# Two feed-forward layers, each taken in two halves of its inner features through one ring of 28 weight slots

## The chip, the cores and the metric

One core of one Trainium2 chip runs the whole program. The metric is the device time of one execution in microseconds (us); lower is better. The kernel before was timed three times, and one further execution was profiled.

## What is computed

Attention with a position bias over 4 batches, 8 heads and 576 positions gives `x`, 2304 tokens of 512 features. Two feed-forward layers follow:

```python
def _moe_ref(x, w_in, w_out):            # d_ff 2048
    h = x @ w_in
    return (h * np.clip(h + 3.0, 0.0, 6.0) / 6.0) @ w_out

def _moe2_ref(x, w_gate, w_val, w_out):  # d_ff 1536
    gate = 1.0 / (1.0 + np.exp(-(x @ w_gate)))
    return (gate * (x @ w_val)) @ w_out
```

## The kernel before

**Stages.** The bias is built and attention runs (to about 367 us), then layer 1 and layer 2. The change touches the two layers and the weight loader alone. Both layers walk over 6 tiles of 384 tokens (`TW`, `NTILE`).

**Layer 1** goes for each tile over 16 blocks `f` of 128 inner features. For a block, `project` issues 12 matmuls (each operand is split in a high and a low part, so 4 chunks times 3 products), `hardswish` makes `g` (ScalarE L535, VectorE L536), `split_g` cuts it in `gh` (ScalarE L566) and `gl` (VectorE L567), and `out1` issues 12 matmuls into four PSUM accumulators. `out1` runs two blocks behind `project`, by the list `pend`. At a tile's end `split_x` makes the next tile's `XH` and `XL` (four ScalarE casts L520, four VectorE subtractions L521), the last two `out1` follow, and the accumulators are copied through two `raw` buffers and written to DRAM as `x2` (L623). The projections of blocks 0 and 1 of the first tile are issued within attention.

**Layer 2** has 12 blocks `e` per tile: two projections (gate and value), sigmoid (ScalarE L645), a product (VectorE L646), `split_g`, and `out2`, nine matmuls of 512 columns, one block behind.

**The weights.** 32 parts for layer 1 (`w_in`, `w_out` in turn), 36 for layer 2 (gate, value, out in turn). They come as 64-bit floats of 128x512 and are turned into a high and a low 32-bit part by a `Loader`. One `tick` starts the DMA of coming parts into `raw` (SyncE queue), takes the magnitude of part `i` on ScalarE (L133) and VectorE (L134) into a `z` buffer, puts part `i-1` together in three VectorE operations (L141, L143, L145), and splits part `i-2` into its slot: a cast on ScalarE (L151) and a subtraction on GpSimd (L152). There are four `z` buffers; a `z` is free when GpSimd is done with it. So a part costs two ScalarE, four VectorE and one GpSimd operation.

**When ticks run.** Ten parts are loaded during attention. All others of layer 1 are loaded in the first tile, at 1.7 ticks a block (`TICK1`). Layer 2 starts loading in layer 1's last tile (1.5 ticks a block up to 16, `TICKS`, `TICKN`), and continues in its own first tile at two ticks a block. In all other tiles no weight is loaded: a layer's parts all stay in SBUF.

All engines run in program order, so an instruction that waits holds up those behind it on its engine.

Of the kernel before, what the change touches and what calls it, by code (L numbers as in the profile page):

```python
# [46 lines left out]
LATE = 3  # L47

TICK1 = 17
TICKS, TICKN = 12, 16  # L50
# [46 lines left out]
def block_kernel(ctx: ExitStack, tc: tile.TileContext, q, k, v, mlp, w_in, w_out, w_gate, w_val, w_out2, dist_d,  # L97
# [12 lines left out]
    x2 = [dram.tile([P, 4, TW], F32, name=f"x2_{t}") for t in range(NTILE)]  # L110

    class Loader:
# [6 lines left out]
        def __init__(self, todo, raw_tile=None):  # L119
            self.todo, self.raw_tile = todo, raw_tile or (lambda i: ring("raw"))  # L120
            self.raw, self.z, self.n, self.sent, self.done = {}, {}, 0, 0, 0

        def dma(self, i):
            if i < len(self.todo) and i == self.sent:
                raw = self.raw_tile(i).rearrange("p r f -> p (r f)").bitcast(I32)
                self.raw[i] = raw.rearrange("p (f w) -> p f w", w=2)
                nc.sync.dma_start(raw, self.todo[i][1].bitcast(I32))
                self.sent += 1
# [32 lines left out]
        def tick(self):  # L161
# [5 lines left out]
            for j in range(i, i + (3 if pools else 2)):  # L167
                self.dma(j)
# [4 lines left out]
    slots2, X2, outs, spare = [], [], [], []  # L173
    pools, turn = [], [0]

    def ring(name):
# [3 lines left out]
        turn[0] += 1  # L180
        if pools and turn[0] % 3 == 0:
            return pools[0].tile([P, 2, 512], F32, name="raw")
        return stg.tile([P, 2, 512], F32, name="raw", bufs=2)

    def slot1(i):
        if len(slots) == i:
            slots.append(pools[0].tile([P, 2, 512], F32R, name=f"slot{i}"))
        return slots[i]

    def raw1(i):  # L190

        if pools and i < 32 - 2 * LATE and i % 2:
            return pools[0].tile([P, 2, 512], F32, name=f"slot{32 - LATE + i // 2 % LATE}")
        return ring("raw")

    def todo(where, parts):
        return [((lambda i=i: where(i)), part) for i, part in enumerate(parts)]

    load1 = Loader(todo(slot1, [w[f] for f in range(NF) for w in (w_in, w_out)]), raw1)
    load2 = Loader(todo(lambda i: slots2[i], [w[e] for e in range(NE) for w in (w_gate, w_val, w_out2)]))  # L200

# [235 lines left out]
    with ExitStack():  # L437
# [95 lines left out]
        def hardswish(f, ph):  # L533
            g = (outs if outs else x1)[f % 2][:, 0:TW]
# [8 lines left out]
        for i in range(NSLOT):  # L543
# [5 lines left out]
            if i in (NS // 2 + 1, NS // 2 + 2):  # L549
                f = len(begun)  # L550
                begun[f] = hardswish(f, project(slots[2 * f], pp.tile([P, 2, 512], F32, name="s")[:, 0]))
            if i % EVERY == 0 and i > 10 and load1.n < NPRE:
                with tc.issue_after(last_v[0].ins):
                    load1.whole()
            if i in PRIME:
                load1.tick()
# [4 lines left out]
        pools.append(moe)  # L561
# [7 lines left out]


        def out1(f, g, os):
            gh, gl = g
            sl = slots[2 * f + 1]
            for r, x in ((0, gh), (1, gh), (0, gl)):
                for c in range(4):
                    nc.tensor.matmul(os[c][:, 0:TW], sl[:, r, P * c : P * c + P], x,  # L576
                                     start=(f == 0 and r == 0 and x is gh), stop=(f == NF - 1 and x is gl))

        def load_x2(t):
            nc.sync.dma_start(X2[t % 2], x2[t])  # L580

        for t in range(NTILE):
            os, pend = [], []
            if t == NTILE - 1:
                for i in range(2):
                    w = keep.tile([P, NT], F32R, name=f"x{i}")
                    slots2 += [w[:, 1024 * j : 1024 * j + 1024].rearrange("p (r f) -> p r f", r=2) for j in range(2)]
                slots2 += slots
                for i in range(2, 4):
                    w = keep.tile([P, NT], F32, name=f"x{i}")  # L590
                    X2.append(w[:, 0 : 4 * TW].rearrange("p (c t) -> p c t", c=4))
                    outs.append(w[:, 4 * TW : 4 * TW + 512])
                    spare += [w[:, 512 * j : 512 * j + 512] for j in range(2)]
                load_x2(0)
            for f in range(NF):
                if t == 0:
                    while load1.done < min(2 * f + 2, 2 * NF):
                        load1.tick()
                g = begun.pop(f) if f in begun else hardswish(f, project(slots[2 * f]))
                if f == 0:  # L600
                    os += [mp.tile([P, 512], F32, name=f"o{c}") for c in range(4)]
                pend.append((f, split_g(g), os))
                if t == 0:
                    while load1.n < min(NPRE + 2 + TICK1 * (f + 1) // 10, 2 * NF + 2):
                        load1.tick()
# [84 lines left out]
```

## Time and profile before

| | us |
|---|---|
| median of 3 runs | 1253.83 (1253.34 to 1255.91) |
| the profiled execution: time / span | 1257.99 / 1256.2 |
| TensorE busy | 1201.4 (96%) |
| VectorE busy | 663.4 (53%) |
| ScalarE busy | 538.3 (43%) |
| GpSimd busy | 284.1 (23%) |

A busy share is a mean over all stages: TensorE can be the engine that sets the end in one tile and wait for another engine in the next. So the stages are read one by one.

### The profile page before, as it was taken

The numbers are of one execution on the slowest core, as the hardware profiler recorded it, in microseconds if no ns is written. First come the engines' busy times: TensorE is split into PE (matmuls) and PEld (weight loads), VectorE is DVE, ScalarE is ACT, GpSimd is POOL, SyncE is SP. The second block draws the span as 40 slices with busy tenths as digits, with TensorE's granted clock in tenths as the row PEclk, the third lists the DMA queues.
The fourth block names the chain that finished last, engine by engine and source line by source line (L and its number), as shares of the span: only waits on it lengthen the run. The fifth ranks groups of instructions, "written<-read, shape, count | busy, mean of one in ns | idle before, by whom it ended". The sixth has DMA issues, their size and how long they took to land.

```text
span 1256.2 us, 18666 instructions
## 1 busy us (share of the span) xinstructions
PE 1201.4 (96%) x7302; PEld 1063.9 (85%) x7302; DVE 663.4 (53%) x1312; ACT 538.3 (43%) x1123; POOL 284.1 (23%) x222
## 2 busy tenths in 40 slices
PE   7889999999998899999999998989999999999998
PEld 3367777776777799999999997978999999999998
DVE  8967777777878932323242499795112121221211
ACT  5867777776854432323232454543112121221211
POOL 4925566655424400000000043231000000000000
PEclk9989999999999999999999999989999999999999
DMA  5643635253233200000010342541001010000000
GB/s 167 231 158 97 184 100 178 87 155 112 74 120 130 84 26 1 26 1 26 1 45 16 109 142 93 186 151 59 9 1 51 1 51 1 1 26 1 26 1 26
DMA packets 31160, 92.60 MB, mean 74 GB/s; under 512 B 3552, under 2 KB 6880, under 8 KB 31072
## 3 DMA queue, kind: packets, MB, share of 16 engines
q1 hardware_dynamic: 31072, 91.41, 22.6%
q8 instruction: 57, 0.93, 0.3%
q14 instruction: 31, 0.25, 0.1%
HBM read 71.35 MB, written 20.05 MB: 73 GB/s over the span
## 4 chain that ended last, share of the span: by engine, by line
PE 76%; DVE 14%; issue 5%; ACT 3%; DMA 1%; POOL 1%; SPq 0%; DVEq 0%; ACTq 0%
PE o L576 11%; PE h L528 11%; PE h L530 11%; PE h L529 11%; PE o L633 11%; PE s L280 6%; PE av L370 5%; PE tr L338 4%; DVE z L143 4%; DVE z L134 2%; DVE z L145 2%; PE s L507 2%; PE av L373 1%; DVE z L141 1%; DVE x L502 1%
## 5 line engine op out<-in xcount | busy, mean ns | idle before, releaser
L529 PE MATMUL h<-early,slot 128*128 128x384 f32 x880 | 294.8, 335 | 0.9 <-POOL slot L152 0.9
L528 PE MATMUL h<-early,slot 128*128 128x384 f32 x880 | 295.5, 336 | 0.1
L530 PE MATMUL h<-early,slot 128*128 128x384 f32 x880 | 294.9, 335 | 0.0
L646 DVE TENSOR_TENSOR g<-g,h 128x384 f32<-128x384 f32 x72 | 39.8, 553 | 251.4 <-PE h L530 250.8
L529 PEld LDWEIGHTS h<-early,slot 128*128 128x128 f32 x880 | 165.6, 188 | 3.9 <-POOL slot L152 1.2
L528 PEld LDWEIGHTS h<-early,slot 128*128 128x128 f32 x880 | 165.8, 188 | 3.3 <-ACT slot L151 0.4
L576 PE MATMUL o<-gh,slot 128*128 128x384 f32 x768 | 151.0, 338 | 16.2 <-ACT gh L566 16.2
L530 PEld LDWEIGHTS h<-early,slot 128*128 128x128 f32 x880 | 165.4, 188 | 0.0
L576 PEld LDWEIGHTS o<-gh,slot 128*128 128x128 f32 x768 | 134.0, 188 | 20.8 <-ACT gh L566 20.7
L152 POOL TENSOR_TENSOR slot<-z,slot 128x512 fp32r<-128x512 f32 x64 | 95.0, 1487 | 181.8 <-ACT slot L151 156.6
L536 DVE SCALAR_TENSOR_TENSOR x<-x,h 128x384 f32<-128x384 f32 x94 | 51.9, 552 | 132.9 <-ACT x L535 132.8
L300 ACT ACTIVATE p<-u,stat 128x576 f32<-128x576 f32 x128 | 98.6, 772 | 46.3 <-DVE stat L284 40.6
L280 PE MATMUL s<-k,q 128*128 128x288 f32 x640 | 114.5, 313 | 0.5 <-DVE stat L284 0.3
L633 PE MATMUL o<-slot,gh 128*128 128x512 f32 x396 | 104.5, 399 | 7.2 <-ACT gh L566 7.2
L535 ACT ACTIVATE x<-h,half 128x384 f32<-128x384 f32 x94 | 54.5, 580 | 130.8 <-PE h L530 130.8
L645 ACT ACTIVATE g<-h 128x384 f32<-128x384 f32 x72 | 35.4, 492 | 174.1 <-PE h L530 172.3
L284 DVE CUSTOM_DVE_ANT_0 u<-s,bias 128x576 f32<-128x576 f32 x128 | 93.5, 753 | 16.0 <-PE s L280 12.1
L566 ACT CAST gh<-g 128x384 fp32r<-128x384 f32 x72 | 36.9, 513 | 132.7 <-DVE g L646 132.7
L280 PEld LDWEIGHTS s<-k,q 128*128 128x128 f32 x640 | 91.2, 193 | 2.5 <-DVE stat L284 0.9
L633 PEld LDWEIGHTS o<-slot,gh 128*128 128x128 f32 x396 | 74.0, 190 | 20.4 <-ACT gh L566 8.2
L576 PE MATMUL o<-gl,slot 128*128 128x384 f32 x384 | 83.7, 339 | 2.1 <-DVE gl L567 2.1
L567 DVE TENSOR_TENSOR gl<-x,gh 128x384 fp32r<-128x384 f32 x96 | 59.4, 619 | 43.8 <-ACT gh L566 43.8
(103 smaller groups left out, 1775.7 us busy)
## 6 DMA issues: line engine op xcount, KB each, us to landing
raw<-in_part_dram SPq DMA_DIRECT2D x61, 512.0 KB, 3.5
nbias<-p SPq DMA_DIRECT2D x18, 576.0 KB, 4.5
early<-in_part_dram SPq DMA_DIRECT2D x32, 288.0 KB, 4.3
bias<-nbias SPq DMA_DIRECT2D x16, 576.0 KB, 6.5
vn<-in_part_dram SPq DMA_DIRECT2D x16, 320.0 KB, 3.1
early<-in_part_dram SPq DMA_DIRECT2D x16, 304.0 KB, 3.7
x<-raw SPq DMA_DIRECT2D x12, 384.0 KB, 3.0
x<-x SPq DMA_DIRECT2D x6, 768.0 KB, 4.1
```

What stands on the lines that cost most here:

```text
L152: nc.gpsimd.tensor_tensor(out=slot[:, 1], in0=z, in1=slot[:, 0].bitcast(F32), op=ALU.subtract)
L280: nc.tensor.matmul(ps[:, a, 0:HS], Q[:, q0 : q0 + P], K[:, r, h, HS * a : HS * a + HS], start=(i == 0), stop=(i == len(mm) - 1))
L284: nc.vector.tensor_tensor_reduce(out=halves(u), in0=ps[:, :, 0:HS], in1=halves(bt), op0=ALU.add, op1=ALU.min, scale=-0.125, scalar=3e38, a ...
L300: nc.scalar.activation(probs(t), us.pop(t), AF.Exp, bias=low[n % 2][:, s : s + 1], scale=-1.0, accum_out=sums[n % 3][:, s : s + 1])
L370: nc.tensor.matmul(ps[64 * h : 64 * h + 64, 0:HS], vt[:, 4 * h + g], ptm[:, h, g, cols], start=(g == 0), stop=False)
L528: nc.tensor.matmul(ps[:, 0:TW], wh, XH[:, c], start=(c == 0), stop=False)
L529: nc.tensor.matmul(ps[:, 0:TW], wl, XH[:, c], start=False, stop=False)
L530: nc.tensor.matmul(ps[:, 0:TW], wh, XL[:, c], start=False, stop=(c == 3))
L535: nc.scalar.activation(g, ph, AF.Relu, bias=half, scale=1.0 / 6.0)
L567: nc.vector.tensor_tensor(out=gl, in0=g, in1=gh.bitcast(F32), op=ALU.subtract)
L576: nc.tensor.matmul(os[c][:, 0:TW], sl[:, r, P * c : P * c + P], x, start=(f == 0 and r == 0 and x is gh), stop=(f == NF - 1 and x is gl))
L633: nc.tensor.matmul(os[i], x[:, P * i : P * i + P], sl[:, r], start=(e == 0 and x is gh and r == 0), stop=(e == NE - 1 and x is gl))
```

## The change

One `Loader` takes all 68 parts in order, and a part goes to slot `i % 28` of a ring (`NALL`), 10 slots of which exist from the start and 18 after attention. Each layer runs twice over the six tiles. Pass 1 takes the first half of the inner features (8 blocks in layer 1, 6 in layer 2), pass 2 the rest. In layer 1 pass 1 writes its sums to DRAM (`part_d`); pass 2 reads them back (`take`) and adds them on VectorE while it empties PSUM. In layer 2 pass 1 leaves its sums in SBUF (`acc`) and pass 2 adds into them there. `XH` and `XL` are now made for 24 half tiles in place of 12 tiles. `go_on` gives one tick a block in the first and last half tile of a pass, one every second block between them, as long as the ring has a free slot; in layer 2 one a block. `freed` counts slots that the last half tile of a pass gives back block by block. `raw` buffers for loading are two now; before there were three and some slots not yet in use.

```diff
-LATE = 3
-TICK1 = 17
-TICKS, TICKN = 12, 16
+NALL = 28
...
         def split(self, i):
             if i in self.z:
-                slot, z = self.todo[i][0](), self.z.pop(i)
+                slot, z = slots[i % NALL], self.z.pop(i)
...
-            for j in range(i, i + (3 if pools else 2)):
+            for j in range(i, i + 2):
                 self.dma(j)
...
+        def go_on(freed, to):
+
+            if load.n - 2 < min(NALL + freed, to):
+                load.tick()
...
+        for part2, t in todo:
             os, pend = [], []
...
+            part = take(part_d[t]) if part2 else None
+            for f in range(NH * part2, NH * part2 + NH):
+                while load.done < 2 * f + 2:
+                    load.tick()
...
-                if t == 0:
-                    while load1.n < min(NPRE + 2 + TICK1 * (f + 1) // 10, 2 * NF + 2):
-                        load1.tick()
...
-                    while load2.n < min(TICKS * (f + 1) // 8, TICKN):
-                        load2.tick()
...
+                freed = 2 * NH * part2
                 if t == NTILE - 1:
+                    freed += max(0, 2 * (f - NH * part2 - 1))
+                if f % 2 == 0 or t == 0 or t == NTILE - 1:
+                    go_on(freed, 68)
...
-                evac("AV"[c % 2], two[:, c % 2, 0:TW], os[c][:, 0:TW])
+                if part2:
+                    nc.vector.tensor_tensor(out=two[:, c % 2, 0:TW], in0=os[c][:, 0:TW], in1=part[:, c], op=ALU.add)
+                else:
+                    evac("AV"[c % 2], two[:, c % 2, 0:TW], os[c][:, 0:TW])
                 if c % 2 == 1:
-                    nc.sync.dma_start(x2[t][:, c - 1 : c + 1], two[:, :, 0:TW])
+                    nc.sync.dma_start((x2 if part2 else part_d)[t][:, c - 1 : c + 1], two[:, :, 0:TW])
...
-                if t == 0:
-                    load2.tick()
-                    load2.tick()
...
+                freed = 2 * NF + 3 * NH * part2
+                if t == NTILE - 1:
+                    freed += 3 * (e - NH * part2)
+                go_on(freed, 68)
...
             for i in range(NB):
...
+                o = acc[NB * t + i]
+                if part2:
+                    nc.vector.tensor_tensor(out=o, in0=o, in1=os[i], op=ALU.add)
+                    nc.sync.dma_start(out[TW * t + P * i : TW * t + P * i + P, :], o)
+                else:
+                    evac("AV"[i % 2], o, os[i])
```

The order of VectorE's queue in layer 1's first tile, before, from one block's `hardswish` (L536) to the next:

```order
L536 SCALAR_TENSOR_TENSOR x1_64<-x1_64,h_4420 128x384
L141 TENSOR_SCALAR z_4405<-z_4405 128x512
L134 TENSOR_SCALAR z_4447<-z_4447 128x512
L143 SCALAR_TENSOR_TENSOR z_4405<-slot29_4350,z_4405 128x512
L567 TENSOR_TENSOR gl_4436<-x1_64,gh_4435 128x384
L145 SCALAR_TENSOR_TENSOR z_4405<-slot29_4350,z_4405 128x512
L141 TENSOR_SCALAR z_4447<-z_4447 128x512
L134 TENSOR_SCALAR z_4458<-z_4458 128x512
L143 SCALAR_TENSOR_TENSOR z_4447<-raw_4392,z_4447 128x512
L536 SCALAR_TENSOR_TENSOR x0_63<-x0_63,h_4473 128x384
```

The same place after the change, where the lines are L514 for `hardswish`, L545 for `gl`, and L132, L139, L141, L143 for the four operations of a part:

```order
L514 SCALAR_TENSOR_TENSOR g_4409<-g_4409,h_4410 128x384
L141 SCALAR_TENSOR_TENSOR z_4406<-raw_4362,z_4406 128x512
L545 TENSOR_TENSOR gl_4426<-g_4409,gh_4425 128x384
L143 SCALAR_TENSOR_TENSOR z_4406<-raw_4362,z_4406 128x512
L132 TENSOR_SCALAR z_4448<-z_4448 128x512
L139 TENSOR_SCALAR z_4448<-z_4448 128x512
L141 SCALAR_TENSOR_TENSOR z_4448<-raw_4404,z_4448 128x512
L514 SCALAR_TENSOR_TENSOR g_4451<-g_4451,h_4452 128x384
```

Between two blocks stood seven operations of parts, and now there are five; on average it is four.

VectorE after the change where the first half tile ends, with the last block's `hardswish` (`g_4493`) and `gl_4510` among the operations of two parts and the `split_x` subtractions (L500), and then the first copy out of PSUM (L309):

```order
L500 TENSOR_TENSOR early_4154<-x1_64,early_4154 128x384
L139 TENSOR_SCALAR z_4490<-z_4490 128x512
L500 TENSOR_TENSOR early_4154<-x2_65,early_4154 128x384
L514 SCALAR_TENSOR_TENSOR g_4493<-g_4493,h_4494 128x384
L141 SCALAR_TENSOR_TENSOR z_4490<-raw_4446,z_4490 128x512
L132 TENSOR_SCALAR z_4532<-z_4532 128x512
L545 TENSOR_TENSOR gl_4510<-g_4493,gh_4509 128x384
L143 SCALAR_TENSOR_TENSOR z_4490<-raw_4446,z_4490 128x512
L500 TENSOR_TENSOR early_4154<-x3_66,early_4154 128x384
L139 TENSOR_SCALAR z_4532<-z_4532 128x512
L141 SCALAR_TENSOR_TENSOR z_4532<-raw_4488,z_4532 128x512
L309 COPY raw_4567<-o1_4252 128x384
```

Before, the end of the first tile had no part left to load beside it:

```order
L521 TENSOR_TENSOR early<-x_63,early 128x384
L521 TENSOR_TENSOR early<-x_64,early 128x384
L521 TENSOR_TENSOR early<-x_65,early 128x384
L521 TENSOR_TENSOR early<-x_66,early 128x384
L536 SCALAR_TENSOR_TENSOR x_64<-x_64,h 128x384
L567 TENSOR_TENSOR gl<-x_64,gh 128x384
L330 COPY raw<-o_4226 128x384
```

So the end of this half tile now shares VectorE with two parts.

SyncE's queue after the change at that place, where L125 loads a part, L606 writes sums and L555 reads them back:

```order
L125 DMA raw_4488<-in_part5_dram 128x1024
L125 DMA raw_4530<-in_part4_dram 128x1024
L606 DMA part0_90<-raw_4567 128x2x384
L606 DMA part0_90<-raw_4571 128x2x384
L125 DMA raw_4604<-in_part5_dram 128x1024
L125 DMA raw_4666<-in_part4_dram 128x1024
L555 DMA take_6115<-part0_90 128x1536
```

Before, the writes of a tile's sums (L623) stood behind all of the layer's parts:

```order
L127 DMA raw_4657<-in_part4_dram 128x1024
L127 DMA raw_4699<-in_part5_dram 128x1024
L623 DMA x2_0_84<-raw_4930 128x2x384
L623 DMA x2_0_84<-raw_4934 128x2x384
L623 DMA x2_1_85<-raw_5446 128x2x384
L623 DMA x2_1_85<-raw_5450 128x2x384
```

The loads now stand on both sides of the writes, and share two `raw` buffers with them.

## Rows read from the trace of the kernel before

**Rows 1.** Busy time by stage: window, its us, engines, granted clock, DMA share, GB/s.

```profile
core 0: us, PE busy (x) PEld busy (x) DVE busy (x) ACT busy (x) POOL busy (x), PEclk, DMA share, GB/s
367.40:447.20 79.80, 67.90 (x363) 63.64 (x362) 72.15 (x113) 40.96 (x77) 35.84 (x22) 0.98 0.26 86
447.20:513.80 66.60, 66.60 (x386) 66.60 (x385) 20.93 (x39) 20.41 (x40) 0.00 (x0) 1.00 0.04 13
713.50:790.60 77.10, 69.74 (x385) 66.10 (x385) 68.02 (x107) 38.75 (x73) 24.61 (x17) 1.00 0.39 130
790.60:876.80 86.20, 79.00 (x398) 72.53 (x397) 68.35 (x103) 37.19 (x68) 26.56 (x18) 0.96 0.38 127
...
952.00:1252.50 300.50, 300.45 (x1584) 281.39 (x1582) 62.45 (x113) 58.40 (x118) 0.00 (x0) 1.00 0.04 15
```

**Rows 2.** The chain that ended last: start us, us, what.

```profile
507.55 6.24 PE o L576 x36
...
707.23 6.24 PE o L576 x36
...
872.73 4.12 PE o L633 x18
...
947.85 4.12 PE o L633 x18
```

**Rows 3.** Timeline, layer 1's first matmul after attention: start us, us, instruction, [idle before].

```profile
367.36 0.55 PE L528 MATMUL h<-early,slot 128*128 128x384 f32 x1
```

**Rows 4.** Who waited for whom, first tiles of layer 1 and layer 2: us, times, longest.

```profile
PE o L576 <- ACT gh L566: 9.8, 6, 2.4
...
PE o L633 <- ACT gh L566: 7.2, 3, 2.8
...
ACT z L133 <- POOL slot L152: 16.1, 11, 3.7
```

**Rows 5.** Timeline of one stall in the first tile.

```profile
375.97 4.17 POOL L152 TENSOR_TENSOR slot<-z,slot 128x512 fp32r<-128x512 f32 x1 [3.49 <-ACT slot L151]
...
380.17 0.67 ACT L133 ACTIVATE z<-slot 128x512 f32<-128x512 f32 x1 [3.70 <-POOL slot L152]
...
384.70 1.66 PE L576 MATMUL o<-gh,slot 128*128 128x384 f32 x8 [2.38 <-ACT gh L566]
```

**Rows 6.** Timeline, operations of a part on VectorE and GpSimd in that tile.

```profile
375.49 0.43 DVE L134 TENSOR_SCALAR z<-z 128x512 f32<-128x512 f32 x1
375.82 0.69 DVE L143 SCALAR_TENSOR_TENSOR z<-raw,z 128x512 int32<-128x512 int32 x1
376.42 0.43 DVE L141 TENSOR_SCALAR z<-z 128x512 int32<-128x512 int32 x1
376.76 0.69 DVE L145 SCALAR_TENSOR_TENSOR z<-raw,z 128x512 int32<-128x512 int32 x1
...
391.64 1.29 POOL L152 TENSOR_TENSOR slot<-z,slot 128x512 fp32r<-128x512 f32 x1 [2.75 <-ACT slot L151]
...
394.53 1.77 DVE L143 SCALAR_TENSOR_TENSOR z<-slot,z 128x512 int32<-128x512 int32 x1
```

**Rows 7.** VectorE groups in the first tile's window: busy us, mean ns.

```profile
L134 DVE TENSOR_SCALAR z<-z 128x512 f32<-128x512 f32 x19 | 10.8, 568 | 0.4 <-ACT z L133 0.4
```

**Rows 8.** Timeline, VectorE and ScalarE where a tile ends: layer 1, then layer 2.

```profile
572.97 2.12 DVE L521 TENSOR_TENSOR early<-x,early 128x384 fp32r<-128x384 f32 x4 [0.60 <-ACT early L520]
...
580.05 1.02 DVE L330 COPY raw<-o 128x384 f32<-128x384 f32 x2 [3.35 <-PE o L576]
583.15 0.56 DVE L536 SCALAR_TENSOR_TENSOR x<-x,h 128x384 f32<-128x384 f32 x1 [2.08 <-ACT x L535]
...
951.78 0.69 DVE L330 COPY x<-o 128x512 f32<-128x512 f32 x1 [1.87 <-PE o L633]
```

**Rows 9.** DMA issues of the page: count, KB, median us from issue to landing.

```profile
raw<-in_part_dram SPq DMA_DIRECT2D x61, 512.0 KB, 3.5
...
x<-raw SPq DMA_DIRECT2D x12, 384.0 KB, 3.0
```

More of the change, by code (lines that the diff above doesn't have):

```diff
@@ L110, in block_kernel, with __init__ @@
     x2 = [dram.tile([P, 4, TW], F32, name=f"x2_{t}") for t in range(NTILE)]
+    part_d = [dram.tile([P, 4, TW], F32, name=f"part{t}") for t in range(NTILE)]
     class Loader:
-        def __init__(self, todo, raw_tile=None):
-            self.todo, self.raw_tile = todo, raw_tile or (lambda i: ring("raw"))
+        def __init__(self, todo):
+            self.todo = todo
             self.raw, self.z, self.n, self.sent, self.done = {}, {}, 0, 0, 0
@@ L179, in ring @@
             return stg.tile([P, 512], F32, name="z", bufs=4)
-        turn[0] += 1
-        if pools and turn[0] % 3 == 0:
-            return pools[0].tile([P, 2, 512], F32, name="raw")
         return stg.tile([P, 2, 512], F32, name="raw", bufs=2)
[L185 to L200, printed above, removed]
+    load = Loader([w[f] for f in range(NF) for w in (w_in, w_out)]
+                  + [w[e] for e in range(NE) for w in (w_gate, w_val, w_out2)])
     attn = ExitStack()
@@ L531, in project, with hardswish @@
             return ps[:, 0:TW]
[L533 to L534 removed]
+        def hardswish(g, ph):
             nc.scalar.activation(g, ph, AF.Relu, bias=half, scale=1.0 / 6.0)
@@ L560, in block_kernel @@
         mp = ctx.enter_context(tc.tile_pool(name="mp", bufs=1, space=PSUM, reuse_waits="tile"))
-        pools.append(moe)
+        slots += [moe.tile([P, 2, 512], F32R, name=f"slot{i}") for i in range(NPRE, NALL)]
         def split_g(g):
@@ L568, in split_g, with take, out1 @@
             return gh, gl
-        def out1(f, g, os):
+        def go_on(freed, to):
+            if load.n - 2 < min(NALL + freed, to):
+                load.tick()
+        def take(src):
+            x = moe.tile([P, 4, TW], F32, name="take", bufs=2)
+            nc.sync.dma_start(x, src)
+            return x
+        def out1(f, g, os, first, last):
             gh, gl = g
-            sl = slots[2 * f + 1]
+            sl = slots[(2 * f + 1) % NALL]
             for r, x in ((0, gh), (1, gh), (0, gl)):
@@ new lines, in out1 @@
+                                     start=(first and r == 0 and x is gh), stop=(last and x is gl))
+        NH = NF // 2
+        todo = [(part2, t) for part2 in range(2) for t in range(NTILE)]
+        X2 = None
+        for part2, t in todo:
+            os, pend = [], []
+            part = take(part_d[t]) if part2 else None
+            for f in range(NH * part2, NH * part2 + NH):
+                while load.done < 2 * f + 2:
+                    load.tick()
+                g = begun.pop(f) if f in begun and t == 0 else None
+                if g is None:
+                    g = hardswish(moe.tile([P, TW], F32, name="g", bufs=2), project(slots[2 * f % NALL]))
+                if not os:
@@ L626, in block_kernel, with out2 @@
         NB = TW // P
-        def out2(e, g, os, last=False):
+        acc = [keep.tile([P, NT], F32, name=f"x{i}") for i in range(NPAIR)]
+        acc = [x[:, 512 * j : 512 * j + 512] for x in acc for j in range(4)]
+        acc += [moe.tile([P, 512], F32, name=f"acc{i}") for i in range(2)]
+        def out2(e, g, os, first, end, last):
             gh, gl = g
-            sl = slots2[3 * e + 2]
+            sl = slots[(2 * NF + 3 * e + 2) % NALL]
             mm = [(i, x, r) for x, r in ((gh, 0), (gh, 1), (gl, 0)) for i in range(NB)]
@@ L632, in out2 @@
             for i, x, r in sorted(mm, key=lambda m: m[0]) if last else mm:
-                nc.tensor.matmul(os[i], x[:, P * i : P * i + P], sl[:, r], start=(e == 0 and x is gh and r == 0),
-                                 stop=(e == NE - 1 and x is gl))
-        for t in range(NTILE):
+                nc.tensor.matmul(os[i], x[:, P * i : P * i + P], sl[:, r], start=(first and x is gh and r == 0),
+                                 stop=(end and x is gl))
+        NH = NE // 2
+        for j, (part2, t) in enumerate(todo):
@@ L637, in block_kernel @@
             os = [mp.tile([P, 512], F32, name=f"o{c}") for c in range(NB)]
             prev = None
-            for e in range(NE):
-                while load2.done < 3 * e + 2:
-                    load2.tick()
-                pg = project(slots2[3 * e])
-                pv = project(slots2[3 * e + 1])
-                g = moe.tile([P, TW], F32, name="g", bufs=1)
+            for e in range(NH * part2, NH * part2 + NH):
+                while load.done < 2 * NF + 3 * e + 3:
+                    load.tick()
+                s0 = 2 * NF + 3 * e
+                pg = project(slots[s0 % NALL])
+                pv = project(slots[(s0 + 1) % NALL])
+                g = moe.tile([P, TW], F32, name="g", bufs=2)
```

62 lines of the change are left out of this document (18 added, 44 removed).

## The prediction

> **What bounds the kernel now.** I read the busy time by stage first. In the later tiles of both layers TensorE is never idle: 66.60 of 66.6 us in layer 1's second tile, 300.45 of 300.5 us in layer 2's last four. VectorE is then busy 20.93 us of a tile and 62.45 / 4 = 15.6 us. In the three tiles that load weights it is the other way round: VectorE is busy 72.15 of 79.8, 68.02 of 77.1 and 68.35 of 86.2 us, and TensorE has gaps [rows 1]. So the tiles that load are bound by the preparation of weights, the others by TensorE.
>
> How much is lost there follows from the chain that ended last. A tile of layer 1 lasts (707.23 - 507.55) / 3 = 66.56 us, a tile of layer 2 947.85 - 872.73 = 75.12 us, both without gaps [rows 2]. Layer 1's first matmul outside attention starts at 367.36 us [rows 3], and its first tile ends at 507.55 + 6.24 - 66.56 = 447.23 us. These 79.87 us hold 30 of a tile's 32 groups of 12 matmuls (two projections are already done), 62.40 us of work: 17.5 us are lost. From 707.23 + 6.24 = 713.47 us (the last tile of layer 1) to 872.73 + 4.12 = 876.85 us (the first of layer 2) pass 163.38 us for 141.68 us of work: 21.7 us are lost. Together **39.2 us**, all that the feed-forward part can gain. It includes the slower TensorE clock there (granted 0.98 and 0.96, which means short spells at 1.2 in place of 2.4 GHz after gaps).
>
> The waits tell how it is lost. TensorE hardly waits for a weight slot: it waits for `gh`, 9.8 us in layer 1's first tile and 7.2 in layer 2's, and in the first of them ScalarE has waited 16.1 us for GpSimd to free a `z` buffer [rows 4]. One stall shows the link: GpSimd takes 4.17 us for a subtraction, ScalarE's magnitude behind it waits 3.70 us, `gh` stands behind that in ScalarE's queue, and TensorE loses 2.38 us [rows 5]. The same subtraction takes 1.29 us elsewhere, and a VectorE operation of 0.69 us takes 1.77 beside one [rows 6].
>
> **The change, step by step.**
>
> *What it removes.* The 58 parts that are left after attention spread over twelve half tiles. I count from `go_on` and the order: 8 ticks in layer 1's first half tile, 4, 4 and 2 in the next three, none in the fifth, 6 in the sixth; in pass 2 8, 2, then none until 6 in the last; in layer 2 6 and 4, then 5 and 3 where pass 1 ends and pass 2 begins. No forced tick is needed: when a half tile starts, its slots are filled or three blocks ahead. TensorE's matmuls stay the same in number. If VectorE and ScalarE keep up everywhere, all 39.2 us are gained.
>
> *Do they keep up?* A part occupies VectorE for (72.15 - 20.93) / 19 = 2.7 us in the first tile, (68.02 - 20.93) / 17 = 2.8 in the last and (68.35 - 15.6) / 18 = 2.9 in layer 2 [rows 1, 7] (the 19 is the count of L134; 17 and 18 are those of GpSimd's subtractions). One block's own work is `hardswish` and `gl`, each 0.55 us [rows 8], so one tick a block asks 2.8 + 1.1 = 3.9 us of VectorE in 66.56 / 16 = 4.16 us: 94%. Before, 1.7 ticks asked 5.9 us. In layer 2 it is 4.0 us of 6.26. So only half tiles with one tick a block are in question, and there mostly the last block, since `out1` runs two blocks behind and hides a lateness of some 4 us, but the last block's `gl` is needed soon. I count what VectorE's queue holds ahead of that `gl`, against the time it has:
> - layer 1, first half tile: 6.7 parts at 2.7, 14 operations of blocks at 0.55 (six `hardswish`, eight `gl`), three subtractions of `split_x` at 2.12 / 4 = 0.53 [rows 8], 0.5 for the last of attention: 27.9 us. The last `gl` is wanted after six projections, seven `out1` and eight matmuls, 13 x 2.08 + 1.4 = 28.4 us after 367.4 (2.08 = 66.56 / 32).
> - sixth half tile: its ticks begin at the third block, 3 x 2.08 + 0.9 = 7.1 us in, and the `gl` is wanted 0.7 us before its end, at 32.6: 6 parts at 2.9, 11 operations, four subtractions, 25.6 us in 25.5.
> - seventh: its first load waits for the write of the sums, 0.5 to copy, 3.0 to write, 3.5 to load [rows 9], so it starts some 8.3 us in, and has 6.3 parts, 11 operations, four subtractions: 26.5 us in 32.6 - 8.3 = 24.3.
> - twelfth: 5.6 parts, ten operations, four subtractions: 23.9 us in the 24.6 after the third block's `gl`.
>
> With VectorE never waiting the loss is 0.1 + 2.2 = 2.3 us. In the first tile before VectorE stood idle 7.65 of 79.8 us, 9.6%, for the reason in rows 5; with that share all four run over, by 2.4, 2.8, 5.0 and 1.8 us: 12.0 us. At one tick a block a `z` comes round every four blocks (16.6 us; before 9.8), so that wait should be rarer, but the density is near to that tile's: I take 8.5, nearer to the upper end.
>
> *What it adds.* The second pair of sums in the first half tile goes through the buffer of the first, so ScalarE and VectorE wait for a write of 3.0 us before they go on to the next tile's first `gh` and `gl`: copy 0.5, write 3.0, copy 0.5 and `gh` 0.5 are 4.5 us, behind a queue that is some 2 us late, and `out1` wants `gh` 6.24 us after the tile's end (three projections). Behind the seventh half tile four additions take the place of two copies with a part's work ahead of them. I put 1 us on each, 2 us together. Elsewhere VectorE is free from 580.05 + 1.02 to 583.15 us at a tile's end [rows 8]; four additions like the copies (0.51 each) end before that. In layer 2 three additions of 0.69 us (nearest row: the copy) take 2.1 us, and the next product on VectorE needs two projections, 4.16 us. The 12 further `split_x` stand behind 6.24 us of `out1` in layer 1 and 4.12 us in layer 2, as now. If that cover were missing, each would cost about 2 us.
>
> *The sum.* Profiled: 1257.99 - 39.2 + 8.5 + 2 = 1229.3. The median of the runs lies 4.2 us below the profiled execution, so **1225 us**. Bounds: 1253.83 - 39.2 = 1214.6 with nothing left, plus 2.3 = 1217; with 12.0 + 2 lost 1229, and 1231 with 2 us for spells of slow clock after the gaps (0.02 of 79.8 and 0.04 of 86.2 us before, 1.6 and 3.4 us [rows 1]). Two `z` buffers hold the `g` of blocks 0 and 1 at the end of attention, which holds back one magnitude there; I cost it at nothing, since the two-block lag covers it, and a stall like that of rows 5, 2.4 us, if not.
>
> **The rivals.** (1) *All hidden.* The light half tiles and the two-block lag absorb the rest; 1215 to 1219. For it: the loads above are within 2 us of the time there is. Against: the order puts operations of parts ahead of the last `gl`. (2) *GpSimd and VectorE add up in full.* A part's four VectorE operations follow each other in 0.33 + 0.60 + 0.34 + 0.60 = 1.9 us when nothing disturbs them (the last taken like the second); with GpSimd's 1.29 added in full a part costs 3.2 in place of 2.8 [rows 6], 28 parts in the dense half tiles 28 x 0.4 = 11 us more: 1225 + 11 = 1236, and up to 1241 with the upper bound. The Trainium skill, "SBUF — State Buffer", section "Who interferes with whom", has it so: VectorE with two SBUF inputs, or in a two-port mode, and a reading GpSimd exclude each other for a whole instruction. The trace has both sides of that (4.17 for 1.29, 1.77 for 0.69), but a part's mean of 2.8 shows that some of GpSimd's time falls where VectorE does other things. (3) *Slower.* Each of layer 1's 12 ends of half tiles makes the next one wait for the write of the sums (3.0 us), because both `raw` buffers are taken and ScalarE, with `gh` queued behind, waits for a load. It decides from (39.2 - 10.5) / 12 = 2.4 us each; with the whole write exposed everywhere 1225 + 36 = 1261. Against: most of these half tiles load nothing, and the buffers there were written out a tile earlier. (4) *No change.* The preparation costs 58 x 2.8 us wherever it stands, and the loss only moves: 1254. Against: VectorE has 45 us free in a tile without loads.
>
> **How the numbers follow.** Likeliest case, 1219 to 1231: 0.55. All hidden: 0.2. Full sum: 0.17. Slower: 0.05. No change: 0.03. The range 1216 to 1240 leaves out these last two and the ends of (1) and (2), together 0.15 to 0.2. Within 0.2% (2.5 us) is what a measurement of this kernel can't tell from no change. Faster 0.92, same 0.03, slower 0.05.
>
> **What would show it.** In the changed kernel's trace TensorE should be without gaps in all of layer 2, and in layer 1 the first tile of pass 1 should end within about 4 us of 33.3 us a half tile. The remaining waits should be TensorE for `gh` or `gl` at the ends of the first, sixth, seventh and twelfth half tiles, few us each. ScalarE's wait for GpSimd should fall from 16.1 us to a few. The prediction is wrong if TensorE waits for `gh` at the ends of half tiles that load nothing, if ScalarE waits for DMAs of `raw` for more than some us, or if a half tile with eight ticks loses 8 us or more, half of what the first tile loses now.

## The result, and the profile after

The changed kernel takes **1241.05 us** (1240.27 to 1242.48, four runs) against 1253.76 us for the kernel before in the same session: ratio 0.9896, 95% interval 0.9879 to 0.9914. It is faster, as forecast, but by 12.7 us (1.0%) in place of 28.8, and 1 us above the range. The profiled execution took 1240.27 us.

The windows show half tiles of the changed kernel, and answer to [rows 1]: layer 1's first two, its sixth, seventh and twelfth, layer 2's first, and all the rest of layer 2.

```profile
core 0: us, PE busy (x) PEld busy (x) DVE busy (x) ACT busy (x) POOL busy (x), PEclk, DMA share, GB/s
360.70:395.60 34.90, 31.66 (x171) 30.97 (x170) 31.63 (x51) 18.34 (x35) 11.25 (x9) 0.95 0.31 104
395.60:431.30 35.70, 33.84 (x193) 33.20 (x193) 27.45 (x45) 17.66 (x35) 9.00 (x7) 1.00 0.35 118
531.20:569.70 38.50, 35.32 (x193) 34.69 (x192) 29.92 (x47) 19.64 (x38) 12.36 (x9) 0.96 0.31 103
569.70:606.60 36.90, 35.02 (x194) 34.70 (x193) 31.17 (x53) 19.28 (x36) 8.13 (x6) 0.96 0.40 136
739.90:776.70 36.80, 34.51 (x190) 33.87 (x190) 29.11 (x48) 18.67 (x35) 10.86 (x9) 0.96 0.44 151
776.70:821.90 45.20, 40.26 (x202) 37.16 (x202) 35.50 (x56) 18.83 (x34) 10.44 (x8) 0.95 0.46 158
821.90:1233.40 411.50, 411.50 (x2174) 386.27 (x2173) 123.63 (x218) 98.47 (x197) 11.28 (x8) 1.00 0.10 33
```

The matmuls of a half tile take 16 x 2.08 = 33.28 us in layer 1 (29.12 in the first, with two projections done) and 75.12 / 2 = 37.56 us in layer 2 [rows 2]. So these six half tiles lose 5.8, 2.4, 5.2, 3.6, 3.5 and 7.6 us, 28.2 together, and the others next to nothing (the last row: TensorE busy 411.50 of 411.50 us). Before it was 39.2. The border at 776.70 us is where the copies of layer 1's last sums begin; the last matmul of layer 1 ends at 777.58, so with the border there the last two figures are 4.4 and 6.7, with the same total. Of the 28.2, idle time is 17.4 (windows less TensorE's busy time); the other 10.8 are matmuls that ran longer than 33.28 or 37.56 us. The granted clock is 0.95 or 0.96 in the five windows where most of it lies: parts of them ran at 1.2 in place of 2.4 GHz. The share that was not granted, times the length of these five windows, gives an estimate of 8.5 us for the clock.

Who waited for whom from 360 to 850 us, answering to [rows 4] (total, times, longest):

```profile
ACT z L131 <- DMA raw<-in_part_dram: 34.3, 23, 4.9
...
PE o L564 <- ACT gh L544: 12.4, 9, 2.9
...
PE o L619 <- ACT gh L544: 4.9, 1, 4.9
...
ACT z L131 <- POOL slot L150: 1.3, 1, 1.3
```

TensorE still waits for `gh` alone. ScalarE's wait for GpSimd is nearly gone (16.1 us before), as forecast. New is ScalarE's wait for loads, 34.3 us, the sign that the prediction named as its undoing. It was the first suspect.

The largest stall, at the end of layer 2's first half tile, in the timeline:

```profile
801.69 1.41 DVE L545 TENSOR_TENSOR gl<-g,gh 128x384 fp32r<-128x384 f32 x1 [0.64 <-ACT gh L544]
...
806.14 1.29 POOL L150 TENSOR_TENSOR slot<-z,slot 128x512 fp32r<-128x512 f32 x1 [3.45 <-issue]
806.18 1.79 DVE L141 SCALAR_TENSOR_TENSOR z<-raw,z 128x512 int32<-128x512 int32 x1
...
809.43 1.30 POOL L150 TENSOR_TENSOR slot<-z,slot 128x512 fp32r<-128x512 f32 x1 [2.00 <-PE h L509]
...
809.80 1.35 DVE L545 TENSOR_TENSOR gl<-g,gh 128x384 fp32r<-128x384 f32 x1 [0.63 <-ACT gh L544]
811.07 0.42 DVE L132 TENSOR_SCALAR z<-z 128x512 f32<-128x512 f32 x1
...
813.32 0.42 DVE L132 TENSOR_SCALAR z<-z 128x512 f32<-128x512 f32 x1
...
818.00 1.39 PE L619 MATMUL o<-slot,gh 128*128 128x512 f32 x3 [4.94 <-ACT gh L544]
```

Two things are to be seen. Two L132, so two parts, stand between one block's `gl` and the next block: the scheduler drew the ticks of the next half tile forward into the free places of this one. And a VectorE operation of 0.69 or 0.56 us takes 1.79 or 1.35 when GpSimd's subtraction has begun just ahead of it. The two act together: from one block's `gl` (801.69) to the next (809.80) pass 8.11 us, for 6.26 us of matmuls. Without the 0.85 us by which the first `gl` is longer and the 1.10 us of L141 an estimate of 6.2 us is left, which would just fit.

### The profile page after: what moved, and what is told of

Read it like the earlier page. It is cut to its first block, busy times and chain, and to the rows that moved or that the text cites. A ratio compares the mean times of both kernels' runs of the same rounds, so it can differ in the third digit from the quotient of the medians.

```text
span 1238.5 us, 18871 instructions
## 1 busy us (share of the span) xinstructions
PE 1197.9 (97%) x7302; PEld 1065.0 (86%) x7302; DVE 705.5 (57%) x1402; ACT 557.5 (45%) x1171; POOL 274.8 (22%) x222
## 4 chain that ended last, share of the span: by engine, by line
PE 79%; DVE 11%; ACT 4%; DMA 3%; issue 3%; POOL 0%; DVEq 0%; ACTq 0%; SPq 0%; POOLq 0%
PE o L564 12%; PE h L509 11%; PE h L507 11%; PE h L508 11%; PE o L619 11%; PE s L259 6%; PE av L349 5%; PE tr L317 4%; DVE z L141 2%; PE s L486 2%; PE av L352 2%; DMA raw<-in_part_dram 1%; DVE z L143 1%; DVE x L481 1%; DVE z L132 1%
## 5 line engine op out<-in xcount | busy, mean ns | idle before, releaser
L507 PE MATMUL h<-early,slot 128*128 128x384 f32 x952 | 319.0, 335 | 0.0
L509 PE MATMUL h<-early,slot 128*128 128x384 f32 x952 | 318.8, 335 | 0.0
L508 PE MATMUL h<-early,slot 128*128 128x384 f32 x952 | 318.4, 334 | 0.0
L150 POOL TENSOR_TENSOR slot<-z,slot 128x512 fp32r<-128x512 f32 x68 | 91.9, 1352 | 617.7 <-ACT slot L149 352.3
L507 PEld LDWEIGHTS h<-early,slot 128*128 128x128 f32 x952 | 179.2, 188 | 2.7
L508 PEld LDWEIGHTS h<-early,slot 128*128 128x128 f32 x952 | 178.8, 188 | 2.6
L509 PEld LDWEIGHTS h<-early,slot 128*128 128x128 f32 x952 | 178.6, 188 | 0.0
L544 ACT CAST gh<-g 128x384 fp32r<-128x384 f32 x166 | 85.1, 513 | 185.9 <-DVE g L634 125.3
L564 PE MATMUL o<-gh,slot 128*128 128x384 f32 x768 | 154.0, 343 | 12.4 <-ACT gh L544 12.4
L564 PEld LDWEIGHTS o<-gh,slot 128*128 128x128 f32 x768 | 137.7, 192 | 15.3 <-ACT gh L544 15.3
L545 DVE TENSOR_TENSOR gl<-g,gh 128x384 fp32r<-128x384 f32 x166 | 103.5, 623 | 71.9 <-ACT gh L544 70.6
L619 PE MATMUL o<-slot,gh 128*128 128x512 f32 x432 | 112.8, 396 | 4.9 <-ACT gh L544 4.9
L263 DVE CUSTOM_DVE_ANT_0 u<-s,bias 128x576 f32<-128x576 f32 x128 | 93.5, 752 | 12.9 <-PE s L259 11.1
L619 PEld LDWEIGHTS o<-slot,gh 128*128 128x128 f32 x432 | 80.7, 189 | 18.8 <-ACT gh L544 5.4
L513 ACT ACTIVATE g<-h,half 128x384 f32<-128x384 f32 x94 | 54.3, 577 | 92.8 <-PE h L509 92.7
L514 DVE SCALAR_TENSOR_TENSOR g<-g,h 128x384 f32<-128x384 f32 x94 | 51.7, 550 | 70.9 <-ACT g L513 70.9
```

What stands on the lines that cost most here:

```text
L150: nc.gpsimd.tensor_tensor(out=slot[:, 1], in0=z, in1=slot[:, 0].bitcast(F32), op=ALU.subtract)
L263: nc.vector.tensor_tensor_reduce(out=halves(u), in0=ps[:, :, 0:HS], in1=halves(bt), op0=ALU.add, op1=ALU.min, scale=-0.125, scalar=3e38, a ...
L507: nc.tensor.matmul(ps[:, 0:TW], wh, XH[:, c], start=(c == 0), stop=False)
L508: nc.tensor.matmul(ps[:, 0:TW], wl, XH[:, c], start=False, stop=False)
L509: nc.tensor.matmul(ps[:, 0:TW], wh, XL[:, c], start=False, stop=(c == 3))
L544: nc.scalar.copy(gh, g)
```

## The experiments

Four theories. **A**: two raw buffers, shared with the sums; ScalarE waits for loads with `gh` queued behind. **B**: VectorE is full where parts crowd, whoever holds the buffers. **D**: the crowding comes from ticks that are drawn forward, two parts to a block. **G** (rival 2 of the prediction): GpSimd's subtraction lengthens VectorE's operations.

All results in one table. "Lost" is the time from layer 1's first matmul to the last matmul's end in the one profiled execution, less the matmuls' own 62.40 + 5 x 66.56 + 6 x 75.12 = 845.9 us. It leaves out attention, whose end varies: layer 1's first matmul starts at 367.4 us in the kernel before and at 360.7 in the changed one. Ratios are to the kernel before on the same chip.

| kernel | us, median | ratio, 95% interval | lost, us |
|---|---|---|---|
| before | 1253.8 | 1 | 39.2 |
| changed | 1241.1 | 0.9896, 0.9879 to 0.9914 | 28.2 |
| 1 own buffer for the sums | 1255.3 | 1.0004, 0.9985 to 1.0024 | 42.4 |
| 2 four raw buffers, own sums, 26 slots | 1260.8 | 1.0044, 1.0029 to 1.0059 | 45.9 |
| 3 26 slots | 1244.9 | 0.9945, 0.9924 to 0.9965 | 27.5 |
| 4 no loads past part 28 | 1223.4 | 0.9758, 0.9736 to 0.9779 | 7.4 |
| 5 layer 2 paced | 1232.7 | 0.9827, 0.9805 to 0.9849 | 17.9 |
| 6 layer 1 paced | 1225.3 | 0.9759, 0.9732 to 0.9786 | 11.1 |
| 7 both paced | 1216.3 | 0.9708, 0.9693 to 0.9724 | 1.7 |
| 8 both paced, four raw buffers | 1217.4 | 0.9715, 0.9696 to 0.9735 | 2.8 |
| 9 both tied, a tick a block | 1224.8 | 0.9768, 0.9738 to 0.9798 | 10.2 |
| 10 changed, no subtraction | 1216.2 | 0.9705, 0.9690 to 0.9720 | 1.1 |
| 11 before, no subtraction | 1215.5 | 0.9678, 0.9651 to 0.9704 | 0.6 |
| 12 changed, subtraction on VectorE | 1227.3 | 0.9769, 0.9742 to 0.9796 | 2.0 |
| 13 before, on VectorE in the layers | 1222.7 | 0.9755, 0.9732 to 0.9778 | 7.3 |
| 14 changed, on VectorE in the layers | 1214.7 | 0.9691, 0.9669 to 0.9713 | 2.1 |
| 15 as 14, both paced | 1213.9 | 0.9684, 0.9660 to 0.9709 | 0.2 |

**Buffers (1, 2, 3).**

```diff
-                    two = ring("raw")
+                    two = moe.tile([P, 2, TW], F32, name="two", bufs=1)
```

> The sums get a buffer of their own, so the two raw buffers serve loads alone. Theory A (two raw buffers: ScalarE, with the copies gh queued behind, waits for loads that start late because a buffer is still held) puts part of the loss on the sums that take a raw buffer at the end of each of layer 1's half tiles: the first half tile of layer 2 (7.6 us lost) and the second and seventh of layer 1 (2.4 and 3.6 us) shrink, some 3 us in all, 1238 us. Theory B (VectorE is full where two parts fall into a block, whoever holds the buffers): 1240 to 1242 us, no change.

Kernel 2 has this too, takes every second raw buffer from a ring of two more, and `NALL = 26`.

> Four raw buffers for loads and one for the sums, paid for with two slots of the ring (26 in place of 28). Theory A: ScalarE's 25.9 us of waits for raw loads in the three loading stretches go, the loss of some 28 us falls towards the 10.5 us of the prediction, 1224 to 1228 us. Theory B: two parts in a block cost 2 x 2.9 us of VectorE beside 1.1 us of its own in 6.26 us (and 2.9 beside 1.9 in 4.16 us of layer 1), so the waits only change their name and the time stays at 1236 to 1241 us.

Both were slower than the changed kernel, by 14 and 20 us, where A wanted 3 and 13 to 17 us less; B had them unchanged. In kernel 2 ScalarE's wait for loads fell to 6.9 us, and TensorE's wait for `gh` in layer 1 doubled (12.4 us in the changed kernel). ScalarE now waits for GpSimd to free a `z`:

```profile
ACT z L131 <- POOL slot L150: 28.6, 21, 3.1
...
PE o L570 <- ACT gh L550: 24.1, 11, 4.6
...
ACT z L131 <- DMA raw<-in_part_dram: 6.9, 4, 2.4
```

Its windows show why: with loads seldom late VectorE is busy 40.00, 39.31 and 39.90 of 40 us, GpSimd half of the time, and the granted clock is lower still.

```profile
380.00:420.00 40.00, 30.17 (x146) 28.47 (x145) 40.00 (x63) 21.18 (x41) 19.32 (x11) 0.87 0.54 182
560.00:600.00 40.00, 31.45 (x146) 29.33 (x145) 39.31 (x58) 21.88 (x41) 17.50 (x12) 0.83 0.46 152
780.00:820.00 40.00, 31.56 (x151) 28.95 (x150) 39.90 (x65) 19.40 (x35) 18.41 (x10) 0.91 0.62 204
```

So theory A falls, and B was too mild: the two buffers held the crowding back. The control with 26 slots alone:

> The ring has 26 slots and nothing else changes: the control for the kernel with four raw buffers, which took 1261 us. If the four buffers slowed that kernel (they let VectorE be filled without a pause), this one stays at 1240 to 1244 us; if the two missing slots did it, it takes 1250 us or more.

At 1244.9 us it lies just above the forecast for harmless slots. It lost no more than the changed kernel in its profile, so the slots are not the main part of what slowed kernel 2 by 20 us. But its ratio's interval lies above the changed kernel's, by some 6 us of the time; its profiled execution took 1241.4 us, and why its median lies 3.5 us above that is not settled.

**No loads past part 28 (4).** `load.todo` is cut to 28 parts.

> Leaves out every part past the 28th: no load, no assembly; the matmuls read what lies in the slots. If all of the loss lies where parts are prepared, the sixth, seventh and twelfth half tile of layer 1 and the first of layer 2 lose nothing and the first two lose 8 us as now: 1241 less 20, 1221 us. Rival (the halves themselves cost: sums written, read back and added at each half tile's end): half tiles 6, 7, 12 and 13 still lose 2 us each or more and the time stays above 1229 us.

```profile
366.90:402.00 35.10, 30.60 (x174) 29.91 (x173) 32.16 (x51) 18.44 (x35) 11.62 (x9) 1.00 0.32 107
402.00:437.40 35.40, 33.70 (x193) 33.06 (x193) 27.35 (x46) 18.07 (x35) 8.49 (x7) 1.00 0.34 117
437.40:1219.00 781.60, 781.60 (x4290) 754.02 (x4289) 248.14 (x455) 215.06 (x415) 4.07 (x3) 1.00 0.11 36
```

All of the 7.4 us lost lie in the first two half tiles, about as forecast. Behind them TensorE is busy 781.60 of 781.60 us: the sums written, read back and added, and the further `split_x`, cost nothing where no part is prepared beside them.

**Pacing (5, 6, 7, 9).** A tick may not be issued before its own block's sigmoid, or in layer 1 its Relu, and in layer 1 it goes to every second block:

```diff
-                nc.scalar.activation(g, pg, AF.Sigmoid)
+                sg = nc.scalar.activation(g, pg, AF.Sigmoid)
...
-                go_on(freed, 68)
+                with tc.issue_after(sg.ins):
+                    go_on(freed, 68)
...
-                if f % 2 == 0 or t == 0 or t == NTILE - 1:
-                    go_on(freed, 68)
+                if f % 2 == 0 or t == NTILE - 1:
+                    with tc.issue_after(load.last.ins):
+                        go_on(freed, 68)
```

Layer 2 alone (5):

> In layer 2 each tick is tied to follow its block's sigmoid, so that the scheduler can't draw the ticks of the next half tile forward: one part a block in place of two. Theory D (the 7.6 us lost in layer 2's first half tile come from two parts in a block): that half tile takes 38 to 39.5 us in place of 45.2, 1234 to 1236 us in all. Rival: the loss is the start of layer 2 (loads behind the writes of layer 1's last sums, the read of the first tile): the half tile still loses 5 us or more, 1239 to 1241 us.

Layer 1 alone (6):

> Layer 1 paced as in the kernel paced in both layers, layer 2's ticks free to be drawn forward. If the two halves of the pacing add up (1241 to 1232.7 by layer 2, to 1216.3 by both): 1224 to 1226 us, with the loss in the first half tile of layer 2 and the twelfth of layer 1. If ticks freed in one place are drawn into another, less is gained: 1230 us or more.

Both (7):

> The ticks of layer 1 are tied too, each behind its block's Relu, and go to every second block save in the last tile; layer 2 as in the kernel paced there alone. Theory D (the loss is two parts drawn into one block): half tiles 6, 7 and 12 of layer 1, which lost 5.3, 3.6 and 3.5 us, lose under 1 us each, the first two lose 5 to 8 us (their parts are needed at once), and the time falls to 1219 to 1224 us. Rival (each part costs the matmuls some 0.5 us wherever it is put, 28 us over 56 parts): 1230 to 1234 us, as with layer 2 paced alone.

D holds for layer 2's first half tile, which takes 38.0 us in kernel 5, and the two pacings add up: 28.2 us lost became 17.9, 11.1 and 1.7. Kernel 6 lies in its forecast; kernel 7 is better than D forecast: the first two half tiles were to lose 5 to 8 us and lose 1.0. In layer 1 it changes two things at once, the tie and the number of ticks (six in place of eight in the first half tile), so kernel 9 has to tell them apart. Two windows of kernel 7, layer 1's sixth half tile and layer 2's first:

```profile
526.40:559.70 33.30, 33.30 (x194) 33.30 (x193) 26.87 (x46) 17.13 (x34) 7.92 (x6) 1.00 0.35 119
759.40:797.40 38.00, 37.83 (x200) 35.12 (x200) 26.02 (x44) 15.96 (x30) 8.35 (x6) 1.00 0.41 140
```

Kernel 9 keeps the changed kernel's condition on `f` and `t` and only ties the ticks to their blocks:

> Both layers' ticks tied behind the block's Relu or sigmoid, but layer 1 gets its ticks as often as in the changed kernel: one a block in the first and last tile of a pass. Theory E1 (one part a block is harmless, only ticks drawn forward, two in a block, hurt): within 2 us of the kernel with a tick every second block, 1216 to 1218 us. Theory E2 (eight parts in a half tile of layer 1 are too many for VectorE beside GpSimd, however they are placed): half tiles 6 and 7 still lose 3 us each, 1221 to 1226 us.

Its first, sixth and seventh half tiles:

```profile
362.60:397.20 34.60, 31.29 (x171) 30.59 (x170) 32.81 (x52) 17.61 (x34) 11.26 (x8) 0.96 0.36 120
530.80:564.10 33.30, 33.30 (x194) 33.30 (x194) 26.86 (x46) 17.09 (x33) 7.91 (x6) 1.00 0.35 119
564.10:599.90 35.80, 33.65 (x194) 33.24 (x193) 30.60 (x51) 19.71 (x38) 10.52 (x8) 1.00 0.39 125
```

1224.8 us and 10.2 us lost: the total is in E2's range, but not where E2 put it. The sixth half tile (second row) loses nothing with the same six parts that cost the changed kernel 5.2 us: there the tie alone is the whole gain. What is left lies mostly where eight ticks are called: 5.4 us in the first half tile, and 2.5 in the seventh (third row) with 1.2 behind it. In the first half tile VectorE's queue still holds two parts in two of its blocks, so density and crowding are not told apart there. It is the kernel nearest to what the prediction had in mind (one tick a block, where `go_on` calls it), and the prediction gave that 10.5 us and 1225.0.

**Both paced with four raw buffers (8).**

> Both layers paced, and four raw buffers with a buffer for the sums and 26 slots, as in the kernel that took 1261 us. Theory D: with one part to a block the buffers are not what is waited for, within 3 us of the kernel paced in both layers with its two shared raw buffers. Theory A in what is left of it (ScalarE waits for loads): 3 us or more below that kernel. If more buffers fill VectorE by themselves: 10 us or more above it.

Within 1.1 us of kernel 7: paced, the buffers don't matter. This kernel has the same single buffer for the sums as kernel 1 and loses 2.8 us where that lost 42.4, so the single buffer does not by itself cost much. The traces of kernels 1 and 2 show the crowding: in layer 1's sixth and twelfth half tiles VectorE takes up eight parts in kernel 1 and ten in kernel 2 (L132), six in the changed kernel. That free buffers are why more is drawn forward is argued, not shown.

**GpSimd (10 to 15).** Kernels 10 and 11 leave out L150 (L152 before), so they compute something else and serve for timing alone.

> Leaves out GpSimd's subtraction of every part (the matmuls read the high half twice in place of the low half); the order of the other engines stays. If VectorE's operations on a part are lengthened by GpSimd beside them (2.76 us a part on average in the two layers, 2.24 us by the rows without GpSimd), VectorE gets back 0.5 us a part and the loss of 28 us falls by 10 to 15 us, 1226 to 1231 us. If the two hardly disturb each other: 1238 to 1241 us.

> The kernel before, with GpSimd's subtraction of every part left out (the matmuls read the high half twice). If most of its 39.2 us of loss is what GpSimd's subtraction does to VectorE and to the z buffers, it falls to 1220 to 1232 us. If the loss is the density (1.7 to 2 parts in a block, 2.2 us of VectorE each even alone: 4.9 of 4.16 us in layer 1): more than 20 us of loss stay, 1235 us or more.

Both lose about 1 us, far better than either forecast, though their parts crowd as ever: layer 2's first half tile in kernel 10 has nine L132, two a block in four of its blocks, and loses 1.0 us. VectorE's groups from 360 to 850 us (busy us, mean ns), first in the changed kernel:

```profile
L545 DVE TENSOR_TENSOR gl<-g,gh 128x384 fp32r<-128x384 f32 x104 | 67.9, 653 | 42.4 <-ACT gh L544 42.2
L514 DVE SCALAR_TENSOR_TENSOR g<-g,h 128x384 f32<-128x384 f32 x94 | 51.7, 550 | 70.9 <-ACT g L513 70.9
L141 DVE SCALAR_TENSOR_TENSOR z<-raw,z 128x512 int32<-128x512 int32 x52 | 50.1, 964 | 1.3
...
L132 DVE TENSOR_SCALAR z<-z 128x512 f32<-128x512 f32 x52 | 26.4, 509 | 16.8 <-ACT z L131 16.7
```

and in kernel 10, where the first two lines are numbered one less:

```profile
L544 DVE TENSOR_TENSOR gl<-g,gh 128x384 fp32r<-128x384 f32 x108 | 60.2, 558 | 44.1 <-ACT gh L543 43.8
L513 DVE SCALAR_TENSOR_TENSOR g<-g,h 128x384 f32<-128x384 f32 x94 | 51.8, 552 | 78.6 <-ACT g L512 78.6
L141 DVE SCALAR_TENSOR_TENSOR z<-raw,z 128x512 int32<-128x512 int32 x53 | 36.6, 690 | 1.4
...
L132 DVE TENSOR_SCALAR z<-z 128x512 f32<-128x512 f32 x53 | 22.5, 425 | 17.6 <-ACT z L131 16.8
```

`gl`, L141 and L132 are shorter without GpSimd by 0.10, 0.27 and 0.08 us on average; `hardswish`, which reads PSUM beside one tile in SBUF, is not (0.550 and 0.552). And ScalarE still waits for loads for 33.9 us in kernel 10, with 1.1 us lost:

```profile
ACT z L131 <- DMA raw<-in_part_dram: 33.9, 32, 2.1
```

That is the second way in which theory A falls. In the kernel before, without the subtraction, TensorE has no gap in the window of layer 1's first tile, beside [rows 1]:

```profile
364.40:444.00 79.60, 79.60 (x460) 79.55 (x459) 60.17 (x124) 46.98 (x87) 0.00 (x0) 1.00 0.29 96
```

So nearly the whole loss of both kernels goes with GpSimd's subtraction. In the changed kernel that is G, since ScalarE waits only 1.3 us for a `z`. In the kernel before, where that wait was 16.1 us [rows 4], the lengthened operations and the `z` buffers held by GpSimd are not told apart. D and G do not exclude each other: the changed kernel's loss takes both, parts that crowd and GpSimd beside them, and removing either removes most of it (kernels 7 and 14). The next kernels keep the computation whole and move the operation (the first diff is kernel 12's, the second that of 14; 13 asks for `pools` in place of the count):

```diff
-                nc.gpsimd.tensor_tensor(out=slot[:, 1], in0=z, in1=slot[:, 0].bitcast(F32), op=ALU.subtract)
+                nc.vector.tensor_tensor(out=slot[:, 1], in0=z, in1=slot[:, 0].bitcast(F32), op=ALU.subtract)
```

```diff
-                nc.gpsimd.tensor_tensor(out=slot[:, 1], in0=z, in1=slot[:, 0].bitcast(F32), op=ALU.subtract)
+                (nc.vector if len(slots) > NPRE else nc.gpsimd).tensor_tensor(
+                    out=slot[:, 1], in0=z, in1=slot[:, 0].bitcast(F32), op=ALU.subtract)
```

> The changed kernel with each part's subtraction on VectorE in place of GpSimd, order and ticks otherwise the same. If GpSimd's subtraction costs VectorE more than it would cost on VectorE itself: a part loses 0.48 us of lengthening (2.71 to 2.23) and some 0.2 us on the gl beside it and gains 0.7 us, so the loss stays within 5 us of 28 and the time at 1236 to 1244 us. If the two engines hardly disturb each other, VectorE is simply fuller by 0.7 us a part in full half tiles: 1250 us or more.

Better than both forecasts: 2.0 us lost in the layers. But layer 1 began at 373.8 us in place of 360.7, since the ten parts of attention went to VectorE as well (361.9 us in kernel 14, where they do not). With the subtraction moved in the layers alone:

> The kernel before with the subtraction of parts on VectorE in the two layers (GpSimd still does it in attention). If density is what the halves relieve: a part is then 2.23 + 0.69 = 2.9 us of VectorE, the first tile asks 20 x 2.9 + 20.9 = 79 us of it for 62.4 us of matmuls, the last tile and layer 2's first ask as much over, and the time stays at 1245 to 1256 us. If only GpSimd's disturbance is the loss: 1216 to 1230 us.

> The changed kernel with the subtraction of parts on VectorE in the two layers alone. With it on VectorE throughout the two layers took 847.9 us, 1.8 us over their matmuls, and attention 13 us more than in the changed kernel's profile. So 1214 to 1218 us if that carries over; 1222 us or more if GpSimd was kept off for another reason (the order in attention).

> Both layers paced, and the subtraction on VectorE in the layers. The paced kernel lost 1.5 us of the layers' 846.1 us and this can gain no more than that: 1214 to 1217 us. If VectorE is fuller than a block allows (2.9 + 1.1 us of 4.16): 1220 us or more.

The kernel before, otherwise unchanged, falls to 1222.7 us (13), more than the halves gained it. Density was the wrong forecast there: it asked 79 us of VectorE for the first tile, and the tile took 69.5. Of the 7.3 us that are left 7.1 lie in this tile. A window as long as that of [rows 1] now reaches 10 us into the second tile; in it VectorE does 142 operations in place of 113 and is busy less than the 72.15 of 79.8 us:

```profile
367.70:447.50 79.80, 75.57 (x423) 72.93 (x422) 70.26 (x142) 44.46 (x83) 0.00 (x0) 1.00 0.29 96
```

With the halves it is 1214.7 (14): spreading is worth 8.0 us once GpSimd is out of the way, and the intervals of the two ratios are apart. Pacing on top (15) gains nothing that can be told (0.8 us, intervals overlap). Kernels 14 and 15 have the lowest times of those that compute everything, 38 and 39 us below the kernel before, but the intervals of their ratios overlap that of kernel 7, where GpSimd kept the subtraction and the parts were paced.

## Why the prediction was wrong, and what of it held

- *The loss before, 39.2 us.* Right as a bound: kernels 11 and 15 reach 0.6 and 0.2 us.
- *"No forced tick is needed", the adds, the sums, 12 more `split_x`.* Right; the 2 us put on them were zero (kernel 4, and in kernel 10, which loads beside them, the second and the eighth half tile lose nothing).
- *The step that failed: "I count from `go_on` and the order", one tick a block.* The prediction counted how often `go_on` is called in a half tile, and took it that a tick stays in its block. In layer 1 the counts are right to one part, but the queues hold two parts in one block and none in the next; layer 2's first half tile gets nine parts in place of six. There "4.0 us of 6.26", no loss, was by the prediction's own figures 2 x 2.9 + 1.1 = 6.9 of 6.26, and 8.1 in the trace; 7.6 us were lost where TensorE "should be without gaps". In layer 1 four half tiles lost 18.1 us where 8.5 was taken (12.0 the bound), and the second 2.4 where nothing was. The order shown ahead of the prediction had a hint of it: five operations of parts between two blocks, where four is the mean.
- *Tied to their blocks, the same ticks lose 10.2 us (kernel 9; predicted 10.5).* That the totals agree is luck: 2 of the 10.5 us were for additions that cost nothing, and the bound had 2.4, 2.8, 5.0 and 1.8 us for the first, sixth, seventh and twelfth half tiles, where kernel 9 loses 5.4, 0, 2.5 and 0.
- *A part's cost as a mean, 2.8 us.* It hid what decides. A part is 2.23 us of VectorE without GpSimd and 2.71 beside it (the sums of its four operations' means), and the rest falls on `gl`, which TensorE waits for and which the prediction counted at 0.55 us: 0.653 on average, 1.35 and 1.41 in the rows of the largest stall. Rival 2 had the mechanism, which kernels 10, 12 and 14 bear out, and 1236 to 1241 us. That its upper end is the measured time is luck too: its price was 3.2 us a part in layer 1's dense half tiles, where a part took 2.9 in the first of them, and it had no loss in layer 2. The Trainium skill, "SBUF — State Buffer", section "Who interferes with whom", says that, outside its two-port modes, a VectorE instruction with at most one SBUF input does not contend with GpSimd, that one with two contends with a GpSimd instruction that reads SBUF, and that the shared ports are an exclusive lock. The rows agree: `hardswish` 0.550 and 0.552, `gl` 0.653 and 0.558, and the 1.79 us of L141 at 806.18, which are nearly the 1.29 of GpSimd and its own 0.69 added. L132 has one input in SBUF and is longer beside GpSimd all the same (0.509 and 0.425); in which mode it ran no run here shows.
- *ScalarE's wait for loads as the sign of failure.* Wrong as a criterion: kernel 10 waits 33.9 us and loses 1.1, kernel 2 waits 6.9 us and loses 45.9. Two other signs held: ScalarE's wait for GpSimd fell to 1.3 us, and no half tile with eight ticks lost 8 us.
- *Clock.* A term put at nothing in the sum, and at 2 us in the bound. The estimate from the granted clock is 8.5 of the 28.2 us. The granted clock is 1.00 in the windows without gaps. Behind one gap of 2.03 us, at 773.67 us in the trace, eight matmuls take 2.69 us; eight took 1.55 at 766.76.

## What to carry to other kernels

Read the order of an engine's queue, not the number of calls, before saying how dense an operation is, and tie a background operation to the block that it is meant for. A wait that appears after a change need not cost anything: take it away before blaming it, since here it held back worse. Before spreading work because VectorE is full, look at what runs beside it on GpSimd: one operation moved to the fuller engine was worth more (30 us) than a new loop order (13 us). Both together were worth 38 us, and so, within what can be told, was the new loop order with its parts paced (37 us).

## What the hardware showed that was not expected

The same 128x512 subtraction takes 1.36 us on GpSimd (mean of 50 in the changed kernel) and 0.69 on VectorE (kernel 12), and VectorE is busy less when it does it itself (70.26 against 72.15 us). So time in which an operation is held up beside GpSimd stands in the profile as VectorE's busy time: a VectorE that looks full need not be. The Trainium skill, "Perfetto Trace Analysis", section "Optimizing Scalar/DVE Operations", suggests handing work of a saturated VectorE to ScalarE or even GpSimd, and adds that moving it between GpSimd and VectorE might not help because they share an SBUF read port. Here it harmed: the kernel before loses 39.2 us with the subtraction on GpSimd and 7.3 with it on VectorE. In kernel 7 operations are still lengthened, another one now, and it costs next to nothing: L132 takes 844 ns on average from 360 to 850 us, where it takes 425 in kernel 10, and the kernel loses 1.7 us.
